# Copying the inverse transform's result out of PSUM on ScalarE, and pairing the products with q

## The chip, the core and the metric

The kernel runs on one core of one Trainium2 chip. The metric is the device time of one execution in microseconds (us); smaller is better. The kernel before was run eight times: the median is 303.95 us, the lowest 302.06, the highest 305.27. One of these runs, of 302.5 us, was recorded by the hardware profiler.

A core has five engines that run their own instruction streams and meet at semaphores: TensorE (PE in the profile; its weight loads are PEld), VectorE (DVE), ScalarE (ACT), GpSimd (POOL) and SyncE (SP). Transfers are issued from the streams of SyncE, ScalarE and GpSimd.

## The reference, cut to what matters

S is 2048 rows, D is 640 columns, F is 1728; all data are bf16.

```
def _A_ref(q, k, v, shift_k, ssm_k, ssm_D):     # q comes in layer-normed
    k_shift = sum of k shifted by t = 0..3 rows, each times a tap shift_k[:, 3 - t]
    kv = k_shift * v
    y = irfft(rfft(kv padded to 2S) * rfft(ssm_k padded to 2S))[:S]    # causal convolution along the rows
    y = y + kv * ssm_D
    return q * y

def _B_ref(x, w_gate, w_up, w_down):
    return (silu(x @ w_gate) * (x @ w_up)) @ w_down

h  = x + _A_ref(layernorm(x), k, v, shift_k, ssm_k, ssm_D)
h2 = h + _B_ref(layernorm(h), w_gate, w_up, w_down)
```

## The kernel before, in words

**Blocks and halves.** The 2048 rows are cut into four blocks, j = 0 to 3, of 512 rows. Inside a block a row's index is 4p + b: p is the partition (0 to 127), b the row group (0 to 3). The 640 columns are cut into two halves, c = 0 and 1, of CW = 320 columns, so that a half of one row group is one fp32 PSUM tile of 128x320.

**The convolution** is computed block by block in a frequency domain. Block 0 uses dense tables (`dense_c`): forward products of the filter's rows (dfK) and of kv (dfX), a complex product on VectorE (`products`, `combine`), and inverse products (di) which leave the result of two row groups in two PSUM tiles each. Blocks 1 to 3 (`conv_c`) use a two-stage transform: first stage (s1), shuffle by DMA (sh), second stage (s2), complex products with earlier blocks' spectra, inverse second stage (i2), shuffle (rs), inverse first stage (i1). Nearly every TensorE result is copied out of PSUM by `evac`, which may run on ScalarE or VectorE.

**The end of the convolution** is `conv_bp` (lines 1144 to 1166), run for every block, half and pair of row groups `bp`: 16 times. It writes the normalised q rows of two row groups into a tile `qt`, multiplies them by the convolution's result, which stands in PSUM (one product for each row group, line 1153 for block 0, where the scale is applied too, line 1160 for the others), adds both row groups to the rows x in one instruction of 640 columns (line 1164), and takes the statistics for the second layer norm (line 1166, `ln_stats`).

**The FFN.** `ln_bp` normalises the rows (L1006 on VectorE or L1007 on ScalarE) and turns them (line 1199, on TensorE for blocks 0 and 1; by a transposing DMA for blocks 2 and 3). `ffn_f` makes gate and up products, 512 columns wide, for 14 slices of F; `ffn_b` makes the down products, 320 columns wide.

**The shifted k** is made in `kv_block`: four products of the k rows with the four taps (`mul`), added up on VectorE, and the product with v. Each instruction works on four row groups, 1280 columns. Product 0 needs the block's own rows; products 1 to 3 need also three leading rows before each partition's four. For block 0 these are loaded by `load_front` (lines 755 to 783) into `KIN0`: the main rows, cell "m", in one transfer from ScalarE's queue, and the leading rows, cell "h", in two transfers from SyncE's queue (partitions 16 to 127 and 1 to 15). The filter's rows of block 0 (`kraw0c`) come from SyncE's queue too and are turned by TensorE (`k_turn`, line 798).

**What sets the order.** The program records operations with the tiles' cells that they read and write (`Prog.op`). `Prog.schedule` places them on the engines one after the other by readiness and priority; the priorities are the ranks in `_ORDER` (lines 16 to 64), a written list of all operation numbers, and `_WHO` forces an operation that could run on either to ScalarE ("a") or VectorE ("d"). What comes out is a fixed order for every engine and queue. PSUM has eight tiles of 512 fp32 columns: three for the FFN ("pF") and five for the rest ("pC"). A tile can be written again when its last reader is done.

The profile gives most instructions the line of a helper: L681 is a matmul, L664, L665, L667 and L668 are PSUM copies (L664 and L667 on ScalarE, L665 and L668 on VectorE, the last of each with a scale), L672 a transfer, L891 a VectorE tensor_tensor, L997 the power in the layer norm's rstd on GpSimd.

Of the kernel before, what the change touches and what calls it, by code (L numbers as in the profile page):

```python
# [16 lines left out]
59 1571 1566 12 3 1574 93 71 61 1575 1570 73 57 75 67 1567 1535 1534 1538 1586 1551 1203 53 1562 1526 63 1550 1558 1539 1530 1590 1599 1614 1594 6  # L17
1555 1603 1554 1559 1546 1563 1591 1609 1605 1582 1600 1527 84 9 82 137 169 143 145 91 131 102 1531 1543 407 108 151 421 153 90 69 65 100 99 135 160
147 417 409 149 411 419 141 139 162 1585 1604 1601 413 1608 1595 1583 1596 1592 382 1542 122 1610 105 383 386 384 380 1578 119 44 81 158 111 1612 433
211 209 313 78 77 621 449 448 381 95 223 155 393 387 186 232 185 157 414 117 144 152 98 96 138 150 408 221 473 439 136 410 188 109 146 262 412 148 190  # L20
189 83 140 531 40 527 820 573 526 446 477 480 521 41 120 103 62 55 33 74 76 94 58 17 19 1587 1581 114 1613 173 172 511 509 85 164 68 113 528 176 165
460 470 422 512 516 515 514 1547 543 268 517 467 523 469 215 212 216 167 66 35 92 371 174 175 42 106 400 370 166 118 156 385 479 438 415 206 376 192
197 201 193 315 191 401 177 397 529 525 154 101 418 142 182 115 112 471 39 437 38 183 21 273 48 45 10 171 116 121 195 461 459 373 389 178 416 87 16
510 54 168 395 1406 236 202 259 260 133 36 159 198 204 22 196 60 261 513 184 97 0 170 181 72 399 161 420 124 123 402 396 88 234 233 379 37 89 129 64
70 5 14 369 4 7 163 110 28 451 278 454 388 519 434 368 269 398 132 24 179 187 52 372 390 107 545 450 1410 27 25 8 551 1408 1404 764 1418 1426 751 11
194 18 1174 1416 263 256 244 180 31 541 539 303 80 126 435 441 235 283 427 429 47 46 128 465 79 127 1353 1350 86 391 34 483 255 252 23 284 225 537 486
547 306 463 104 26 582 325 227 226 242 29 773 228 32 30 803 377 1252 258 229 253 423 205 43 125 231 50 49 51 264 591 134 1381 213 218 13 466 797 199
207 1382 1251 220 476 214 475 540 222 430 798 200 447 219 203 600 617 643 564 834 311 224 723 431 320 291 506 575 503 568 572 1007 1 285 508 501 474
806 498 272 496 560 668 487 488 953 305 1244 210 1264 505 275 633 1254 337 987 355 394 862 276 628 1256 281 812 814 271 507 570 604 596 296 818 598
295 286 630 810 266 618 310 612 607 876 955 1268 663 1119 580 578 956 631 290 550 1165 577 15 2 1169 1412 499 816 208 392 375 270 436 532 428 468 472  # L30
524 237 217 453 462 442 485 538 542 546 491 481 673 586 1378 1510 655 484 455 544 456 622 280 1520 957 367 795 432 999 552 558 548 440 1109 321 464
920 265 452 518 1248 522 530 627 863 374 592 287 297 579 1258 1009 917 1266 693 799 282 802 1001 1262 944 669 492 609 562 590 566 500 300 494 56 20
327 848 769 444 443 378 497 520 307 808 574 277 245 230 826 445 770 767 1130 968 951 832 1173 1133 240 1015 915 914 243 251 326 974 614 960 856 615
301 585 1227 619 553 536 533 406 424 404 403 594 254 241 819 565 778 602 257 1179 830 426 425 238 713 828 535 583 316 250 334 860 964 1094 1310 490
489 239 405 836 712 707 844 942 1025 783 784 976 554 1092 775 1427 1313 1312 457 1311 534 249 996 776 774 366 841 1083 1068 880 348 978 842 821 768
697 692 1222 555 949 939 247 248 246 274 664 688 708 1060 940 938 677 1022 717 1066 1063 1108 1070 722 1069 796 936 682 947 727 854 329 1037 1036 916
925 1067 932 667 638 636 635 322 567 809 815 1170 1166 1132 962 926 929 1377 927 1026 1011 1005 804 1013 728 931 1020 1231 718 879 1218 1472 924 975
928 1225 1228 933 1012 1124 1078 1354 1419 1144 1349 1290 995 1017 624 866 864 1053 1003 1573 1343 1253 678 1355 1464 946 1260 771 807 559 1113 557
1016 1114 674 1090 1107 1105 1271 805 1272 1129 1141 1458 549 1557 921 292 1606 1456 1549 1580 1569 1462 1588 1593 458 824 1014 587 772 1376 685 793
715 1267 1134 1451 789 1433 1120 794 1018 1615 1584 1401 1403 730 1019 1220 822 1470 1500 1457 792 786 935 788 710 1236 1045 679 1505 1512 1118 881  # L40
714 1317 1273 1513 1511 1178 1415 1235 1440 1187 1503 1239 1508 937 1436 1504 606 952 1116 576 1430 1466 1428 1460 1438 1414 1536 1151 1540 683 347
130 1360 1229 1216 288 997 1448 1315 1006 1142 1226 1522 1117 1523 902 904 1072 726 556 1345 1323 1320 1309 1319 781 1387 1468 877 588 1021 1380 1352
1171 672 1465 1461 1217 782 1177 1154 721 1279 1137 1145 1153 1010 1351 1407 1519 1277 1443 1136 1284 1084 1245 1517 813 684 493 1224 1219 811 504
1265 725 780 972 779 1192 1205 1367 1445 1269 1000 922 1243 843 1242 1241 765 1405 1342 1158 875 1532 1347 620 675 1167 823 716 652 918 734 1399 1064
1041 1579 1495 1560 1556 998 357 923 977 1391 1073 1287 1327 695 1413 1435 1331 747 1112 1493 919 752 1337 1335 1329 1087 676 1223 1299 694 339 748
1123 1373 1291 646 777 1385 671 1307 1221 1397 1389 1285 1122 1409 1402 1270 1027 1043 739 1479 330 954 858 686 1425 743 1131 1143 1086 689 761 1121
1111 1449 1484 1358 1147 1155 1055 1489 1568 1305 738 1076 312 343 1411 1237 1234 1197 984 1446 1474 1156 1359 1471 1431 365 970 1463 658 699 703 900
611 1429 1238 1370 1024 698 966 719 892 980 352 898 660 648 1280 704 1276 599 874 852 657 838 1322 1341 495 1049 1030 502 1292 1293 1033 1450 1469
1368 1452 1082 1240 1184 1577 1518 988 894 896 1497 1363 1364 1477 1475 1476 1051 1398 1157 691 1288 709 1097 1388 666 1442 1437 1396 1149 1128 736
1274 1372 1029 1176 1441 1492 1161 1125 1362 1498 1483 1163 1496 1598 1490 846 1194 681 1275 1190 662 982 1079 1421 994 645 1023 711 705 608 605 1289  # L50
1056 1420 650 361 701 724 1099 1032 1031 309 1052 1281 696 1048 1028 700 1050 943 1059 1494 1193 571 279 1164 1366 318 790 690 1502 589 561 890 1509
1371 878 1507 1196 1152 1482 1375 1140 1374 1189 1333 1038 629 909 1160 886 1480 906 1369 1162 1175 1297 986 1393 1417 641 1499 1200 1439 1054 1127
1453 569 593 1209 1213 1057 1047 1395 1361 1447 1139 642 706 1004 1075 1303 1195 1148 1365 745 1392 1286 934 563 597 1294 1394 1278 1390 1283 1062 702
1040 687 298 289 293 948 945 1039 835 1065 1061 616 1058 1473 1035 1301 756 1295 299 1126 1186 910 1198 869 1501 656 1146 644 1506 1491 868 653 1247
639 871 640 637 1081 1080 887 888 1250 850 872 905 911 908 882 654 1138 833 1042 294 847 595 482 581 829 827 478 845 744 584 304 733 1302 853 855 601
800 613 323 308 1478 907 314 1296 1304 1246 1467 1459 603 867 1211 328 324 1521 1071 735 961 1172 884 885 1100 1386 1089 839 651 625 1597 1282 737
1074 941 746 634 1214 1210 1002 1384 732 731 755 356 1095 1102 1093 973 831 825 1168 1348 1101 1110 1106 1383 1516 319 632 362 959 963 817 837 670
1255 990 665 1257 338 992 1259 967 1541 363 360 623 1098 358 341 344 754 965 1249 883 1328 340 1553 1183 1201 267 912 930 1379 913 1135 1565 801 317
1611 1561 1602 1537 647 359 849 851 785 1545 1529 950 1103 1104 1346 958 865 857 1344 1339 1316 1115 873 891 333 787 1008 840 659 1485 979 1552 1544
1564 1528 1481 1576 1572 903 1336 1199 859 899 971 720 729 1207 861 1159 680 1180 1326 1091 1334 1298 753 983 981 1044 1088 1096 626 610 302 331 985  # L60
969 870 1261 791 901 1321 1318 889 364 346 1185 895 353 332 649 349 342 893 1548 1208 1077 740 1202 1212 1182 1181 760 993 1488 1444 1085 1314 1191
1204 1330 1046 1306 1300 1308 897 345 335 350 1533 354 762 1423 1356 1607 742 758 1150 1263 661 989 991 351 336 1432 1338 1616 1332 1340 1034 1230
1233 1215 1424 1434 1422 1324 757 1589 1514 766 1455 1325 741 1400 750 749 759 1487 1232 1525 1515 1486 1454 1524 1357 1206 1188 763
"""
_WHO = (
# [456 lines left out]
def bass_sequential_preLN__ssm_conv_h3__swiglu_ffn__prompt_kernel(  # L522
# [6 lines left out]
    R = 4  # L529
# [836 lines left out]
```

## Time and profile before

| | us |
|---|---|
| median of eight runs | 303.95 |
| the profiled execution | 302.5 |
| its span, first to last instruction | 300.7 |
| TensorE busy, matmuls | 278.9 |
| VectorE busy | 240.6 |
| ScalarE busy | 194.1 |
| GpSimd busy | 33.5 |

The granted TensorE clock is 0.994 of full speed over the span. Data moved by DMA: 43.24 MB.

The page shows, in this order: busy time of each engine; the span in 40 slices of 7.5 us with the busy share in tenths; the chain of work that ended last, followed back from the last instruction; and the costliest groups of instructions, each with its count, its busy time, the mean ns of one and the idle time before it. Other views answer from the same recorded execution: busy time for any stretch of the span, the timeline of one engine with its idle times in brackets, and the groups with every shape apart. An engine's neighbouring instructions overlap by their pipelines, so the duration of one can be longer than the spacing of two that queue.

### The profile page before, as it was taken

The page shows a single profiled execution, that of the slowest core. Times are in us where ns is not written, and L with a number is a line of the kernel's source. Part 1 is how long each engine was busy: PE and PEld are TensorE (multiplying, and loading weights), DVE is VectorE, ACT ScalarE, POOL GpSimd, SP SyncE. Part 2 cuts the span into 40 slices and gives each one's busy share as a digit, 9 for nine tenths or more (in the row PEclk, how much of TensorE's full clock was granted, in tenths as well). Part 3 has the DMA queues.
Part 4 walks back from the last instruction along what each step waited for, and adds up shares of the span by engine and source line. Part 5 has one row for each costly group of instructions (what it writes and reads, how often), then busy time and mean ns, then how long its engine had stood idle before and what let it go on. Part 6 is the DMA issues. An engine that isn't in the chain of part 4 may idle for free.

```text
span 300.7 us, 5136 instructions
## 1 busy us (share of the span) xinstructions
PE 278.9 (93%) x1786; PEld 151.7 (50%) x1804; DVE 240.6 (80%) x486; ACT 194.1 (65%) x457; POOL 33.5 (11%) x34
## 2 busy tenths in 40 slices
PE   3798897799999989999989999999998999999996
PEld 1465564444543466664433456654444576444564
DVE  3899899998899989999989999984689872323322
ACT  5298899897776857998979985867976010332100
POOL 2103300401101114110160000200030010000000
PEclk9999999799999999999999999999999999999999
DMA  7999997634944796595443204644101124000011
GB/s 215 361 379 342 355 354 240 203 65 158 231 140 116 168 269 191 113 266 173 131 87 83 94 23 143 165 132 156 42 2 44 46 53 122 2 0 0 2 44 44
DMA packets 42472, 43.24 MB, mean 144 GB/s; under 512 B 14848, under 2 KB 37056, under 8 KB 42320
## 3 DMA queue, kind: packets, MB, share of 16 engines
q1 hardware_dynamic: 38974, 38.30, 40.4%
q0 software_dynamic: 3328, 3.97, 8.2%
q10 hardware_dynamic: 146, 0.66, 0.6%
q8 instruction: 14, 0.23, 0.3%
q14 instruction: 10, 0.08, 0.1%
HBM read 20.63 MB, written 2.62 MB: 77 GB/s over the span
## 4 chain that ended last, share of the span: by engine, by line
PE 50%; DVE 35%; DMA 4%; issue 3%; POOL 3%; ACT 2%; SPq 1%; DVEq 0%; ACTq 0%
PE ps L681 49%; DVE sb L891 30%; DMA sb<-sb 3%; POOL stt L997 3%; DVE stt L981 2%; DMA sb<-in_A_ssm_k_dram 2%; DVE sb L665 2%; DVE sb L1153 1%; ACT sb L664 1%; PE ps L1199 1%; ACT sb L1007 1%; SPq L672 1%; ACT sb L667 1%; PE ps L798 0%; DVE sb L1006 0%
## 5 line engine op out<-in xcount | busy, mean ns | idle before, releaser
L681 PE MATMUL ps<-sb 128*128 128x320 bf16 (+2 forms) x1186 | 222.4, 338 | 11.0 <-DMA sb<-in_A_shift_k_dram 2.3
L891 DVE TENSOR_TENSOR sb<-sb 128x1280 bf16<-128x1280 bf16 (+3 forms) x270 | 165.6, 672 | 1.2 <-ACT sb L667 0.8
L681 PEld LDWEIGHTS ps<-sb 128*128 128x128 bf16 (+2 forms) x1204 | 114.3, 99 | 102.2 <-DVE sb L891 5.4
L664 ACT ACTIVATE sb<-ps 128x320 bf16<-128x320 f32 (+2 forms) x257 | 104.2, 482 | 28.5 <-PE ps L681 21.4
L891 DVE TENSOR_TENSOR sb<-ps,sb 128x320 bf16<-128x320 f32 (+2 forms) x70 | 38.9, 572 | 42.6 <-PE ps L681 27.6
L681 PE MATMUL ps<-sb,tab 128*128 128x320 bf16 (+2 forms) x512 | 66.5, 306 | 3.6 <-ACT sb L664 1.7
L1225 ACT ACTIVATE sb<-ps 128x512 bf16<-128x512 f32 (+1 forms) x56 | 33.6, 601 | 37.8 <-PE ps L681 37.3
L681 PEld LDWEIGHTS ps<-sb,tab 128*128 128x128 f16 (+2 forms) x512 | 32.0, 101 | 36.5 <-issue 13.4
L1007 ACT ACTIVATE sb<-sb,stt 128x320 bf16<-128x320 bf16 (+1 forms) x36 | 25.1, 731 | 14.8 <-DVE stt L999 13.4
L997 POOL TENSOR_TENSOR stt<-stt 128x2 f32<-128x2 f32 (+1 forms) x12 | 16.1, 1345 | 115.7 <-DVE stt L996 79.9
L1067 POOL DMA_DIRECT2D sb<-sb x12 | 12.2, 1014 | 74.2 <-DVE sb L891 61.8
L667 ACT ACTIVATE sb<-ps 128x320 bf16<-128x320 f32 x42 | 15.7, 445 | 4.8 <-PE ps L681 4.7
L665 DVE CAST sb<-ps 128x320 bf16<-128x320 f32 x29 | 13.4, 481 | 5.5 <-PE ps L681 5.5
L981 DVE BATCH_NORM_STATS2 stt<-sb 128x6 f32<-128x320 bf16 x32 | 14.3, 477 | 0.0
L1027 ACT ACTIVATE sb<-sb,stt 128x640 bf16<-128x640 bf16 x16 | 13.2, 827 | 0.2
L1020 ACT ACTIVATE sb<-sb 128x640 bf16<-128x640 bf16 x16 | 12.0, 748 | 0.1
L798 PE MATMUL ps<-sb 128*128 128x128 bf16 (+1 forms) x48 | 4.0, 231 | 3.4 <-DMA sb<-in_A_ssm_k_dram 2.3
L809 POOL TENSOR_TENSOR sb<-sb 1x320 bf16<-1x320 bf16 x2 | 3.6, 1796 | 21.4 <-ACT sb L664 14.6
L798 PEld LDWEIGHTS ps<-sb 128*128 128x128 bf16 (+1 forms) x48 | 3.2, 120 | 5.0 <-DMA sb<-in_A_ssm_k_dram 2.9
L1006 DVE TENSOR_SCALAR sb<-sb,stt 128x320 bf16<-128x320 bf16 (+1 forms) x12 | 4.6, 400 | 0.1
L1199 PE MATMUL ps<-sb 128*128 128x128 bf16 x40 | 3.8, 242 | 1.0 <-DVE sb L1006 1.0
L999 DVE TENSOR_TENSOR stt<-stt 128x2 f32<-128x2 f32 (+1 forms) x12 | 1.8, 148 | 3.1 <-POOL stt L997 3.1
(23 smaller groups left out, 29.5 us busy)
## 6 DMA issues: line engine op xcount, KB each, us to landing
sb<-sb SPq DMA_DIRECT2D x72, 160.0 KB, 2.2
sb<-sb POOLq DMA_DIRECT2D x12, 320.0 KB, 4.4
out_dram<-sb SPq DMA_DIRECT2D x16, 160.0 KB, 1.8
sb<-in_A_k_dram SPq DMA_DIRECT2D x8, 280.0 KB, 4.6
sb<-in_B_w_down_dram SPq DMA_DIRECT2D x13, 160.0 KB, 6.3
sb<-cst_den SPq DMA_DIRECT2D x8, 256.0 KB, 6.4
sb<-in_A_v_dram SPq DMA_DIRECT2D x6, 320.0 KB, 3.9
sb<-in_A_q_dram SPq DMA_DIRECT2D x6, 320.0 KB, 3.7
```

The source lines that it names most:

```text
L664: fns = {"act": lambda a: a.activation(out=dst(), in_=src(), func=ACTF.Copy), "dve": lambda v: v.tensor_copy(out=dst(), in_=src())}
L665: "dve": lambda v: v.tensor_copy(out=dst(), in_=src())}
L667: fns = {"act": lambda a: a.activation(out=dst(), in_=src(), func=ACTF.Copy, scale=scale), "dve": lambda v: v.tensor_scalar(out=dst(), in0 ...
L681: return lambda t: t.matmul(o(), l(), r(), start=st, stop=sp)
L891: return lambda v: v.tensor_tensor(out=o(), in0=a(), in1=b_(), op=op)
L981: vec(dve1(CW, False), lambda v: v.bn_stats(st6(l, j, b, c), V(xt, b * D + c * CW, CW)), [(xt, (b, c))], [(ST, ("s", l, j, b, c))], prio, ...
L997: P.op({"pool": 1.2}, lambda g: g.tensor_tensor(out=y, in0=va, in1=stt[:, 420:420 + hi - lo], op=ALU.pow), c1 + [(ST, "half")], c3, prio, ...
L1007: "act": lambda a: a.activation(out=dst(), in_=src(), func=ACTF.Identity, scale=rs(l, j, b), bias=tmv(l, j, 3)[:, b:b + 1])},
L1020: P.op({"act": act_c(D) + 0.22}, lambda a, b=b, jt=jt: a.activation(out=V(jt, 0, D), in_=V(xt, b * D, D), func=ACTF.Copy, accum_out=tmv(l, ...
L1027: P.op({"act": act_c(D) + 0.3}, lambda a, b=b, jt=jt: a.activation(out=V(jt, 0, D), in_=V(xt, b * D, D), func=ACTF.Square, bias=tmv(l, j, ...
L1067: P.op({"pool": 1.35}, [lambda g: g.dma_start(v4(t0), src(), accum_op=ALU.add)], [(t0, 0)] + cells, [(t0, 0)], prio, dma=(2.1, 2.1, 0.8), ...
L1225: P.op({"act": act_c(n)}, lambda a: a.activation(out=dst(), in_=src(), func=ACTF.Silu), rd, wr, -1000, name=f"si{nm}", after=after)
```

## The change

In `conv_bp` the product with q no longer reads PSUM. Each of the two PSUM results is copied by ScalarE to bf16 (for block 0 with the scale), into SBUF that is free by then: `KIN0` for block 0, the shuffled tile `HTt` for the others. Then one VectorE instruction multiplies both row groups, 640 columns, from SBUF. In `load_front` the main and the leading k rows of block 0 are each loaded in two column halves, with cells for each half, so that the products of half 0 depend on half 0 alone. SyncE issues four transfers for the leading rows, ScalarE two for the main rows; pieces are 640 bytes long. `_ORDER` and `_WHO` are replaced by new lists for the new set of operations; the lists are left out here.

```
-            dma([kin(0, 128, 3, 7)], 655, [], [(KIN0, "m")], -2001, name="kin0", w=2.6, eng="act")
-            dma([kin(16, 128, 0, 3), kin(1, 16, 0, 3)], 490, [], [(KIN0, "h")], -2000, name="kin0h", w=2.0)
+            dma([kin(16, 128, 0, 3, 0), kin(1, 16, 0, 3, 0)], 245, [], [(KIN0, "h0")], -2002, name="kin0h", w=1.1)
+            for c in range(2):
+                dma([kin(0, 128, 3, 7, c)], 328, [], [(KIN0, f"m{c}")], -2001 + 2 * c, name=f"kin0", w=1.4, eng="act")
+            dma([kin(16, 128, 0, 3, 1), kin(1, 16, 0, 3, 1)], 245, [], [(KIN0, "h1")], -2000, name="kin0h", w=1.1)
...
+            ot, ob, os_ = (KIN0, bp * 2 * D + c * CW, D) if ready else (HTt, bp * 4 * CW, 2 * CW)
             for k in range(2):
+                oc = [(ot, ("o", c, bp * 2 + k))]
                 if ready:
                     pk = [ready[k]]
-                    vec(dve1(CW), lambda v, k=k, pk=pk: v.scalar_tensor_tensor(out=V(qt, k * CW, CW), in0=B32(pk, 0, CW), scalar=SCALE, in1=V(qt, k * CW, CW),
-                                                                             op0=ALU.mult, op1=ALU.mult), tc(pk) + [(qt, k)], [(qt, k)], pr, name=f"o{j}{c}{bp}")
                 else:
...
-                    vec(dve1(CW), tt(lambda k=k: V(qt, k * CW, CW), lambda pk=pk: B32(pk, 0, CW), lambda k=k: V(qt, k * CW, CW), ALU.mult),
-                        tc(pk) + [(qt, k)], [(qt, k)], pr, name=f"o{j}{c}{bp}")
+                evac(lambda k=k: V(ot, ob + k * os_, CW), lambda pk=pk: B32(pk, 0, CW), CW, tc(pk), oc, pr, scale=SCALE if ready else None,
+                     name=f"oe{j}{c}{bp}", only="act")
+            vec(dve2(2 * CW), tt(lambda: V2(qt, 0, CW, 2, CW), lambda: V2(ot, ob, os_, 2, CW), lambda: V2(qt, 0, CW, 2, CW), ALU.mult),
+                [(ot, ("o", c, bp * 2 + k)) for k in range(2)] + [(qt, 0), (qt, 1)], [(qt, 0), (qt, 1)], pr, name=f"o{j}{c}{bp}")
```

## The prediction

> **What bounds the kernel now.** I read the page's engine shares and slices first, then busy time by stretch, then the chain that ended last, the groups with each shape apart, and VectorE's timeline of the first microseconds.
>
> ```profile
> PE 278.9 (93%) x1786; PEld 151.7 (50%) x1804; DVE 240.6 (80%) x486; ACT 194.1 (65%) x457; POOL 33.5 (11%) x34
> ...
> DVE  3899899998899989999989999984689872323322
> ACT  5298899897776857998979985867976010332100
> DMA  7999997634944796595443204644101124000011
> ```
>
> Up to about 175 us VectorE has no free slice, and the DMA engines are full up to about 50 us. TensorE looks busy everywhere, so its share says little; the stretches say more. I cut them at the first FFN product (60.78), at the first FFN product of block 2 (198.8) and at TensorE's last (297.6); the points come from matching the built program's order with the trace.
>
> ```profile
> core 0: us, PE busy (x) PEld busy (x) DVE busy (x) ACT busy (x) POOL busy (x), PEclk, DMA share, GB/s
> 0.00:9.20 9.20, 3.96 (x20) 1.76 (x20) 3.09 (x6) 4.32 (x10) 1.65 (x8) 1.00 0.77 224
> 9.20:60.78 51.58, 42.58 (x308) 27.00 (x308) 50.18 (x115) 42.95 (x106) 9.82 (x7) 0.97 0.96 320
> 60.78:198.80 138.02, 134.50 (x884) 70.44 (x892) 133.25 (x258) 111.83 (x269) 18.33 (x16) 1.00 0.56 145
> 198.80:297.60 98.80, 97.53 (x579) 52.52 (x585) 53.58 (x110) 34.96 (x74) 3.71 (x3) 1.00 0.14 44
> ```
>
> From 9.2 to 60.78 VectorE works 50.2 of 51.6 us. In gapless stretches late in the trace a 512-column matmul starts every 0.216 us and a 320-column one every 0.137 us. With those spacings TensorE's order holds 37.6 us of work ahead of the first FFN product and 223.5 us from it to the end. It starts that product at 60.78, so 23.2 us are lost before it; the rest takes 236.8 us, so 13.3 are lost after, 11.1 of them before 198.8 (126.9 us of work in 138.0). From 198.8 on, 96.6 us of work fill 98.8. So the end is: when FFN work begins, plus 223.5, plus what TensorE still loses. VectorE sets the first term.
>
> The chain that ended last gives the spacing of instructions that queue back to back:
>
> ```profile
> 49.43 0.78 DVE sb L891
> 50.21 1.20 DVE sb L1153 x3
> 51.41 0.40 DVE sb L891
> 51.81 0.40 DVE sb L1153
> ...
> 225.53 1.29 ACT sb L667 x4
> ```
>
> A 320-column product read from PSUM (L1153) costs VectorE 0.40 us, and so does the 640-column bf16 addition at 51.41; a copy on ScalarE costs 0.32. The durations are longer, since neighbours overlap:
>
> ```profile
> L664 ACT ACTIVATE sb<-ps 128x320 bf16<-128x320 f32 x219 | 83.8, 454 | 18.9 <-PE ps L681 17.8
> ...
> L891 DVE TENSOR_TENSOR sb<-sb 128x640 bf16<-128x640 bf16 x64 | 29.9, 481 | 0.1
> ...
> L665 DVE CAST sb<-ps 128x320 bf16<-128x320 f32 x29 | 13.4, 481 | 5.5 <-PE ps L681 5.5
> ...
> L1153 DVE SCALAR_TENSOR_TENSOR sb<-ps,sb 128x320 bf16<-128x320 f32 x8 | 3.6, 483 | 0.0
> ```
>
> **Part 1, the pair of row groups.** VectorE loses 32 products of 0.40 and gains 16 of 0.40: 6.4 us less. ScalarE gains 32 copies: 10.3 us at 0.32, 14.5 at 0.454. Of all PSUM copies of this shape VectorE keeps 32 of 35 and ScalarE takes 296 after 261.
>
> The Trainium skill speaks against part 1: "ScalarE: Activation LUTs", Rules for kernel authors, puts plain arithmetic on VectorE, in bf16 up to about three times faster. Going by that, the copy belongs on VectorE at a third of 454, 0.15 us; two copies and the product would cost it 0.70, still under the present 0.80, and ScalarE nothing. The rows deny it: VectorE's copy from PSUM takes 481 against ScalarE's 454 and is spaced 0.40, so two copies and a product would be 1.20. I go by the rows: only ScalarE makes it pay.
>
> **Part 2, the new order.** The order list is replaced whole, so I compared the built orders and added, along VectorE's, each kind's spacing (0.735 for 1280 columns, 0.40 for 640 or a PSUM read of 320, 0.23 for 320 in bf16). Up to VectorE's first normalised rows, which the first transposition for the FFN waits for (56.15), the sum falls from 47.4 to 44.0: four pairs -1.6, four PSUM copies given to ScalarE -1.6, one tap copy -0.4, a normalisation +0.3, the rest small. Up to the last copy before the first FFN product it falls from 51.3 to 46.8: two products of block 2 move behind it (-1.5), a copy comes ahead (+0.4). So -4.5 us. ScalarE's sum to that point goes from 42.2 to 41.5 and stays under VectorE's, so it is not the next bound there.
>
> TensorE's order holds 1.0 us less ahead of that product and 1.0 more behind it (224.5). From there to block 2's first, VectorE's sum goes from 131.8 to 127.2, ScalarE's from 103.6 to 106.7, TensorE's from 126.9 to 126.1. The 138.0 measured is 6 over VectorE's sum, so it could shorten by between 0 and 4.6; TensorE is nearly as full and follows waits, so I take 1.0.
>
> **Part 3, the first k rows.** VectorE's start now:
>
> ```profile
> 5.10 0.49 DVE L665 CAST sb<-ps 128x320 bf16<-128x320 f32 x1 [2.53 <-PE ps L681]
> 5.51 0.81 DVE L891 TENSOR_TENSOR sb<-sb 128x1280 bf16<-128x1280 bf16 x1
> 8.79 0.49 DVE L665 COPY sb<-ps 128x640 bf16<-128x640 bf16 x1 [2.47 <-PE ps L798]
> ```
>
> The 2.47 us wait is for filter rows that landed at 7.33. The second product stands behind it because the leading k rows landed at 9.11. With column halves the filter rows stand first in SP's queue, no 82 KB ahead, and 328 instead of 655 KB beside them on ScalarE's queue; the leading rows of half 0 are 244 KB. The second product moves ahead of the wait. That is worth 0.7 at least, and up to 2.3 if the filter rows land 1.6 sooner; a loss is bounded by the tap row, now second on ScalarE's queue (0.4). Pieces of 640 bytes take 34 ns against 203 for 5120, 1.3 times as long per byte: at most 0.5 us on a half. I take 1.0. SP issues two more transfers, some 1.0 us, while it runs far ahead of the landings.
>
> **The floor under this.** In both orders the loads amount to some 15.2 MB before the shuffles of block 1's first spectrum, which landed at 47.9 to 49.2 with the DMA engines full since 9 us. TensorE takes small products and 12 transposes (about 1.5 us) between them and the first FFN transposition, so that cannot come before about 50.7. I expect it at 56.15 - 3.4 - 1.0 = 51.75: just free of the floor.
>
> **GpSimd.** By the skill's "SBUF — State Buffer", Who interferes with whom, a VectorE instruction with two SBUF inputs shuts out a GpSimd one that reads SBUF. The trace agrees: L997 takes 2.93 us at 31.75, beside products from SBUF, and 0.70 at 54.09, beside statistics. The 16 new products have two SBUF inputs. By the rule each of 12 such steps could wait 0.40, 4.8 in all; but VectorE waits for GpSimd 3.1 us in all now, and pairing halves the number of these products. I count 0, within -0.5 and +1.
>
> **Sum.** First FFN product at 60.78 - 4.5 - 1.0 = 55.3; plus 224.5; plus 13.3 - 1.0 lost; the end of TensorE's work at 292.1 instead of 297.6: 5.5 us less. The profiled execution took 302.5 (span 300.7, 1.8 around it), so 297.0; the median of the runs, 303.95, lies 1.45 above it, so 298.45, say 298.5.
>
> **Rivals.**
> - The transfers hold the front: the filter rows of block 1 move from 8.9 to 12.8 MB down the queue (landed 30.0; a transfer at 13.0 MB landed at 40.8), and TensorE takes their transposes between the second and third inverse products of column half 1, at about 40. A late landing stalls TensorE, then VectorE. For it: the full DMA slices. Against: my expected times just clear. It leaves a gain of 1 to 3 us: 302.
> - The middle loosens as well: VectorE's 4.6 less counts almost whole. Against: TensorE has 126 us of work there. 295.
> - ScalarE's copies hold TensorE (slower): from 60.78 to 198.8, 16 of the copies stand in ScalarE's strict order while a PSUM bank is held, and VectorE's paired product waits for two of them. It decides when ScalarE, now 111.8 of 138.0 busy, has no free moment when a bank fills. 0.5 us at each of 16 is 8.0, which turns -5.5 into +2.5: 306.5. For it: its slices between 120 and 175 us are nearly full. Against: its order sum rises by only 3.1.
>
> **Chances.** Likeliest 0.52, transfers 0.20, looser middle 0.14, ScalarE 0.14. A measurement tells 0.5% from no change, 302.4 to 305.5. Of the transfers' case 0.12 lies below it and 0.08 within: faster 0.78, same 0.08, slower 0.14. The range, 294.5 to 304.0, takes in the middle's bound and the transfers' case and leaves out most of the slower one.
>
> **What would show it.** Right: the first FFN product at 54 to 57; VectorE's wait near 8 us gone or under 1.5; VectorE busy 5 to 8 us less in all, ScalarE 7 to 14 more; the 138 us stretch no longer than 138. Wrong: a stall of TensorE near 40 us on a DMA; more TensorE waits on ScalarE than the 10.3 us now (PE and its weight loads on L664); a wait for GpSimd above 4 us.

## The result and the profile after

| | before | after |
|---|---|---|
| median of the runs, us | 303.75 (32 runs, 301.89 to 305.95) | 298.96 (11 runs, 298.11 to 301.95) |
| ratio, 95% interval | | 0.9852 [0.9823, 0.9882] |
| profiled execution, us (span) | 302.5 (300.7) | 299.76 (297.9) |
| first FFN product, us | 60.78 | 59.48 |
| first FFN product of block 2, us | 198.8 | 194.8 |
| end of TensorE's work, us | 297.6 | 294.7 |

The change made the kernel faster by 4.8 us, 1.5%. Unless said otherwise, "after" is a profiled execution of the changed kernel at full granted clock, since an earlier one had 6.8 us of half clock in it, as we will see below. One run of the changed kernel beside the experiments, of 303.06 us, counts as slow (over 1.5% above the fastest) and is left out of the figures below.

The first view is the page's list of busy times, then the busy time of each engine in the same four stretches as in the prediction (boundaries moved with the three events in the table).

```profile
PE 276.7 (93%) x1785; PEld 152.0 (51%) x1804; DVE 235.5 (79%) x473; ACT 200.0 (67%) x486; POOL 35.6 (12%) x34
```

```profile
0.00:9.16 9.16, 3.82 (x20) 1.75 (x20) 3.11 (x6) 4.32 (x10) 1.71 (x8) 1.00 0.82 233
9.16:59.48 50.32, 42.05 (x300) 25.61 (x300) 46.00 (x104) 41.07 (x107) 9.22 (x5) 1.00 1.01 320
59.48:194.80 135.32, 131.50 (x873) 70.95 (x883) 129.97 (x252) 114.38 (x285) 21.68 (x18) 1.00 0.56 143
194.80:294.70 99.90, 98.97 (x595) 53.67 (x602) 55.88 (x113) 40.23 (x87) 2.98 (x3) 1.00 0.18 53
```

In the second stretch VectorE works 46.00 us where it worked 50.18: the order removed 4.2 us of its work ahead of the FFN, nearly what was counted. Yet the stretch is only 1.3 us shorter. VectorE's idle time in it rose from 1.4 to 4.3 us. The third stretch is 2.7 us shorter. The last is 1.1 longer; by the sums of the prediction it holds 1.8 us more of TensorE's work (224.5 - 126.1 = 98.4, against 96.6). The sum is -2.9 us at TensorE's end.

Even the 1.3 us is not won where the prediction had most of it. VectorE's first normalised rows, which the first FFN transposition waits for, start at the same time in the kernel before (L1006) and after (L1010):

```profile
55.65 0.45 DVE L1006 TENSOR_SCALAR sb<-sb,stt 128x640 bf16<-128x640 bf16 x1
```

```profile
55.67 0.45 DVE L1010 TENSOR_SCALAR sb<-sb,stt 128x640 bf16<-128x640 bf16 x1
```

From the first addition of products (10.05 before, 9.39 after) to these rows VectorE works 42.0 us instead of 44.4, but it waits 4.3 instead of 1.2.

The groups with each shape apart show the moved work. The 16 new products of 640 columns stand in the first line (64 before), the copies in the other two (219 and 42 before).

```profile
L895 DVE TENSOR_TENSOR sb<-sb 128x640 bf16<-128x640 bf16 x80 | 37.4, 481 | 2.1 <-ACT sb L665 1.8 <-ACT sb L668 0.2
...
L665 ACT ACTIVATE sb<-ps 128x320 bf16<-128x320 f32 x246 | 93.5, 461 | 21.8 <-PE ps L682 21.1
...
L668 ACT ACTIVATE sb<-ps 128x320 bf16<-128x320 f32 x50 | 19.1, 449 | 1.8 <-PE ps L682 1.7
```

**Where the front's gain went.** The longest idle time of VectorE between 9.2 us and the first FFN product can be followed through four engines. VectorE's timeline after, with the idle time before a piece and its releaser in brackets:

```profile
25.86 4.30 DVE L895 TENSOR_TENSOR sb<-sb 128x1280 bf16<-128x1280 bf16 x8
32.89 0.17 DVE L1000 TENSOR_SCALAR stt<-stt 128x4 f32<-128x4 f32 x1 [2.73 <-ACT sb L1031]
```

ScalarE's timeline, then TensorE's and GpSimd's:

```profile
31.61 0.44 ACT L665 ACTIVATE sb<-ps 128x320 bf16<-128x320 f32 x1 [3.39 <-PE ps L682]
31.95 0.82 ACT L1031 ACTIVATE sb<-sb,stt 128x640 bf16<-128x640 bf16 x1
```

```profile
30.86 8.32 PE L682 MATMUL ps<-sb 128*128 128x320 bf16 x60 [3.24 <-POOL sb L813]
```

```profile
25.75 5.06 POOL L813 TENSOR_TENSOR sb<-sb 1x320 bf16<-1x320 bf16 x1 [14.90 <-ACT sb L665]
```

Read backwards: VectorE waits for a statistics step of ScalarE; that step stands behind a copy of a product; the product waits for an addition on GpSimd. This is `d_add` (`name="dadd"`), which adds the D row to one row of the turned filter, 320 values on one partition, before the forward products of half 1. It takes 5.06 us and ends 0.65 us after VectorE's last product (30.16). In the kernel before the same addition took 2.38 us and TensorE waited 0.35 for it:

```profile
25.28 2.38 POOL L809 TENSOR_TENSOR sb<-sb 1x320 bf16<-1x320 bf16 x1 [14.63 <-ACT sb L664]
```

```profile
27.71 7.24 PE L681 MATMUL ps<-sb 128*128 128x320 bf16 x52 [0.35 <-POOL sb L809]
```

Its other instance, for half 0, took 1.22 us in both kernels. Why the two differ so is taken up at the end.

**The start.** VectorE's first work after:

```profile
7.51 1.56 DVE L895 TENSOR_TENSOR sb<-sb 128x1280 bf16<-128x1280 bf16 x2 [4.93 <-ACT sb L665]
8.98 0.48 DVE L666 COPY sb<-ps 128x640 bf16<-128x640 bf16 x1
9.39 3.00 DVE L895 TENSOR_TENSOR sb<-sb 128x1280 bf16<-128x1280 bf16 x3
```

The two waits of 2.53 and 2.47 us have become one of 4.93: the tap row now lands later, behind half of the main k rows on ScalarE's queue, so that TensorE's tap products wait 5.2 us for it instead of 2.3. The filter copy no longer waits, and the first addition of products starts at 9.39 instead of 10.05. Of these 0.66 us some 0.4 come from the tap copy (L665 at 5.10 before), which VectorE no longer makes.

**The clock.** The page's row of granted clock, by slices of 7.5 us, of the kernel before and of the earlier profile of the changed kernel (302.32 us):

```profile
PEclk9999999799999999999999999999999999999999
```

```profile
PEclk9999599999999999999999999999999999999999
```

In the trace these are stretches of 3.41 us, or two of them in a row, in which TensorE had half its clock. In the kernel before it is this one, with the stretch ahead of it (PEclk stands behind POOL's busy time):

```profile
52.37:55.78 3.41, 1.72 (x18) 0.92 (x17) 3.41 (x18) 2.63 (x8) 0.85 (x2) 1.00 0.40 150
55.78:59.19 3.41, 3.04 (x22) 1.68 (x22) 3.36 (x8) 3.41 (x8) 2.38 (x3) 0.50 0.82 253
```

The mean clock of each run tells how many such steps it had ahead of the last microseconds. All runs of the two kernels whose clock is on record, those beside the experiments among them, sorted by it:

| granted clock | steps of 3.41 us | before: runs, median | after: runs, median |
|---|---|---|---|
| 1.000 | 0 | none | 10, 298.7 |
| 0.994 | 1 | 12, 302.4 | 5, 300.0 |
| 0.989 | 2 | 13, 303.5 | 2, 302.1 |
| 0.983 | 3 | 15, 305.1 | none |

At one step each, the changed kernel is 2.4 us ahead, at two steps 1.4 (from two runs). The 2.7 us between the two profiled executions are no cleaner: the one of before had one step, the one after none. So about half of the 4.8 us, or less, is the gain at equal clock; the rest goes with the clock, since the changed kernel mostly runs with no such step, and the kernel before with one to three. An estimate: 3.41 us at half clock withhold at most 1.7 us of TensorE's time, so where two rows differ by 2.1, the step alone isn't all of it.

### The profile page after: what moved, and what is told of

The parts are those of the page before. It is cut to its first block, busy times and chain, and to the rows that moved or that the text cites. A ratio compares the mean times of both kernels' runs of the same rounds, so it can differ in the third digit from the quotient of the medians.

```text
span 300.5 us, 5153 instructions
## 1 busy us (share of the span) xinstructions
PE 279.6 (93%) x1785; PEld 153.4 (51%) x1804; DVE 235.4 (78%) x473; ACT 199.9 (67%) x486; POOL 35.6 (12%) x34
## 4 chain that ended last, share of the span: by engine, by line
PE 48%; DVE 22%; issue 13%; ACT 7%; POOL 5%; DMA 4%; SPq 0%; ACTq 0%; DVEq 0%; POOLq 0%
PE ps L682 48%; DVE sb L895 19%; ACT sb L665 3%; DMA sb<-sb 3%; ACT sb L1011 2%; POOL stt L1001 2%; POOL sb L813 2%; DVE sb L666 1%; DMA sb<-in_A_shift_k_dram 1%; DVE stt L985 1%; ACT sb L668 1%; DVE sb L1010 0%; ACT sb L1231 0%; POOL sb L1071 0%; SPq L673 0%
## 5 line engine op out<-in xcount | busy, mean ns | idle before, releaser
L895 DVE TENSOR_TENSOR sb<-sb 128x1280 bf16<-128x1280 bf16 (+3 forms) x286 | 172.1, 661 | 12.4 <-ACT sb L665 9.3
L665 ACT ACTIVATE sb<-ps 128x320 bf16<-128x320 f32 (+1 forms) x283 | 113.5, 489 | 29.7 <-PE ps L682 24.1
L682 PE MATMUL ps<-sb,tab 128*128 128x320 bf16 (+2 forms) x512 | 63.5, 302 | 2.2 <-ACT sb L665 0.8
L895 DVE TENSOR_TENSOR sb<-ps,sb 128x512 bf16<-128x512 f32 (+2 forms) x46 | 28.1, 618 | 42.6 <-PE ps L682 34.8
L1011 ACT ACTIVATE sb<-sb,stt 128x320 bf16<-128x320 bf16 (+1 forms) x31 | 22.1, 741 | 10.6 <-DVE stt L1003 8.1
L668 ACT ACTIVATE sb<-ps 128x320 bf16<-128x320 f32 x50 | 19.1, 449 | 1.8 <-PE ps L682 1.7
L813 POOL TENSOR_TENSOR sb<-sb 1x320 bf16<-1x320 bf16 x2 | 6.3, 3135 | 22.4 <-ACT sb L665 15.2
L1010 DVE TENSOR_SCALAR sb<-sb,stt 128x320 bf16<-128x320 bf16 (+1 forms) x17 | 6.6, 414 | 0.3
L1000 DVE TENSOR_SCALAR stt<-stt 128x2 f32<-128x2 f32 (+1 forms) x12 | 1.9, 159 | 3.3 <-ACT sb L1031 3.3
L1031 ACT ACTIVATION_READ_ACCUMULATOR sb<-sb,stt 128x1 f32 x16 | 3.8, 239 | 0.0
```

Of the source, the lines that this page charges most:

```text
L665: fns = {"act": lambda a: a.activation(out=dst(), in_=src(), func=ACTF.Copy), "dve": lambda v: v.tensor_copy(out=dst(), in_=src())}
L668: fns = {"act": lambda a: a.activation(out=dst(), in_=src(), func=ACTF.Copy, scale=scale), "dve": lambda v: v.tensor_scalar(out=dst(), in0 ...
L682: return lambda t: t.matmul(o(), l(), r(), start=st, stop=sp)
L813: P.op({"pool": 1.0}, lambda g: g.tensor_tensor(out=V(kt, 0, CW, 0, 1), in0=V(kt, 0, CW, 0, 1), in1=V(DROW, c * CW, CW, 0, 1), op=ALU.add) ...
L895: return lambda v: v.tensor_tensor(out=o(), in0=a(), in1=b_(), op=op)
L1011: "act": lambda a: a.activation(out=dst(), in_=src(), func=ACTF.Identity, scale=rs(l, j, b), bias=tmv(l, j, 3)[:, b:b + 1])},
```

## The experiments

Each is a full kernel. The order of work on each engine is written down and held, save for the instructions that an edit adds, drops or moves. All were timed beside the kernel before; ratios are to it.

**1. The changed kernel once more.** No edit.

> The changed kernel itself, for a second recorded execution: the first was among its slowest (302.3 us at a granted clock of 0.987, where most of its runs took 298.1 to 299.8). Theory of the prediction (less VectorE work ahead of the first FFN product): at a full clock that product starts at 55 to 58 us and the run takes 299. Rival (the front gained nothing; the stretch from the first FFN product to block 2's is what shrank): it starts at 60 us or later in this execution too, the stretch takes 133 to 135 us instead of 138.0, and the run takes 299 just the same.

299.76 us (298.52 to 300.17), ratio 0.988 [0.984, 0.992]. The lines above are from this run. The first FFN product at 59.48 misses the 55 to 58 of the theory; the stretch behind it, 135.3, lies just outside the rival's 133 to 135. The rival comes nearer: most of the gain is in that stretch. In the earlier profile, with two steps of half clock near 30 us, that product came at 62.75 and the stretch took 134.6.

**2. The pairing alone.** The kernel before with part 1; the two products become one at the place of the later, each copy stands in ScalarE's order at the moment its result was ready.

```
-                    vec(dve1(CW), tt(lambda k=k: V(qt, k * CW, CW), lambda pk=pk: B32(pk, 0, CW), lambda k=k: V(qt, k * CW, CW), ALU.mult),
...
+                evac(lambda k=k: V(ot, ob + k * os_, CW), lambda pk=pk: B32(pk, 0, CW), CW, tc(pk), oc, pr, scale=SCALE if ready else None,
...
+            vec(dve2(2 * CW), tt(lambda: V2(qt, 0, CW, 2, CW), lambda: V2(ot, ob, os_, 2, CW), lambda: V2(qt, 0, CW, 2, CW), ALU.mult),
```

> Part 1 alone: the order of the kernel before is kept on every engine; the 32 copies are put into ScalarE's order where the inverse's result is ready, and the paired product stands where the later of the two products stood. The k rows are loaded whole. Theory of the prediction: VectorE is 6.4 us shorter, 1.6 of it ahead of the first FFN product and about 3 more in the stretch behind it: 300.5 to 302.5. Rival (only the rewritten order pays): 303 to 305. Rival (ScalarE's copies hold up TensorE): 305 to 308.

307.7 us, ratio 1.015 [1.010, 1.019]: slower. VectorE's timeline of this kernel shows the price; each line begins with a paired product, and what follows it on the same helper line is counted in. The first is block 1's half 0:

```profile
85.40 1.70 DVE L891 TENSOR_TENSOR sb<-sb 128x640 bf16<-128x640 bf16 x4 [2.47 <-ACT sb L664]
114.44 1.70 DVE L891 TENSOR_TENSOR sb<-sb 128x640 bf16<-128x640 bf16 x4 [3.18 <-ACT sb L664]
```

Before, the four products at this place started at 81.17, 81.68, 82.32 and 82.73, each as its bank came. Now the first pair needs both banks and both copies: its last inverse product ends at 83.6, the last two copies start at 84.92 and 85.24 behind others on ScalarE, and the product starts at 85.40. In the list of waits VectorE's L891 waits 12.7 us in all for copies of ScalarE's L664, a line that the list of before doesn't have, and the stretch from the first FFN product to block 2's takes 141.2 us instead of 138.0. It isn't the clock: at 0.989 this kernel has 307.5, the one before 303.5. The time lies in the range of the second rival, that ScalarE's copies hold up TensorE. That is a smaller part of it by the waits: TensorE's for L664 grew from 10.3 us to 13.8 (PE and weight loads), VectorE's from nothing to 12.7.

**3. Pairing alone, paired products moved back.** The code of 2, with VectorE's list changed at four places: the paired products of block 0 half 1 (first pair), block 1 half 0 (first pair) and half 1 (second pair), and block 2 half 1 (first pair), with what depends on them, stand behind 0.9, 2.5, 3.2 and 1.2 us of VectorE work that doesn't. Block 0's copies stand just ahead of their use in ScalarE's list.

```
-o100, o101, h100, h101
+(2.5 us of other work), o100, o101, h100, h101
```

> Part 1 alone in the order of the kernel before, as in pair_alone (307.7), but with the places chosen for it: four of the paired products, with what depends on them, move behind independent VectorE work that is as long as VectorE waited there (0.9, 2.5, 3.2 and 1.2 us), and the copies for block 0 stand just ahead of their use. Theory (the paired product puts the inverse product, two copies and two hops in front of VectorE, and only an order made for it hides that): 301 to 304, most of the loss gone. Rival (ScalarE's extra copies are the loss): 306 to 308 as before.

310.98 us, ratio 1.024 [1.020, 1.028]: slower still, outside the theory's range and the rival's. My theory of the wait alone fell. Waits as long return before paired products (2.98 us at 88.76, 3.09 at 118.81), and the first FFN product comes at 64.6 (62.5 in experiment 2; this profile had three steps of half clock ahead of it, that one two, so the difference is not the order's alone). This local repair of the order doesn't do; what a better one would give was not tried.

**4. The order alone.** The changed kernel with its order and its k halves, but the products as before, one each, straight from PSUM. Seven inverse products had to be moved to where q is ready, since their banks would not be free otherwise.

```
-                evac(lambda k=k: V(ot, ob + k * os_, CW), lambda pk=pk: B32(pk, 0, CW), CW, tc(pk), oc, pr, scale=SCALE if ready else None,
...
+                    vec(dve1(CW), tt(lambda k=k: V(qt, k * CW, CW), lambda pk=pk: B32(pk, 0, CW), lambda k=k: V(qt, k * CW, CW), ALU.mult),
```

> Parts 2 and 3 without part 1: the changed kernel's order and k loads, but each row group's result is multiplied straight from PSUM, two products on VectorE near the places where the copies stood. Seven of the inverse products of blocks 2 and 3 had to move back to where the q rows are normalised, since nothing else frees their PSUM tile. Theory of the prediction: VectorE gets the 6.4 us back, and the run takes 302.5 to 305.5. Rival (the rewritten order pays by itself): 299 to 300.5.

307.88 us, ratio 1.016 [1.011, 1.021]: slower as well, above both ranges, by 3.0 us at a clock of 0.989. Because of the seven moves it is not quite the order by itself. First FFN product at 64.0, the stretch after it 137.5; its profile has two steps of half clock near 30 us, as the earlier one of the changed kernel, which had 62.75 and 134.6. TensorE's weight loads wait 13.0 us for VectorE's L895, against 7.0 in the changed kernel. The addition on GpSimd takes 5.04 us here, so its length comes with the order, not with the pairing.

**5. The copies on VectorE.** The changed kernel with

```
-                     name=f"oe{j}{c}{bp}", only="act")
+                     name=f"oe{j}{c}{bp}", only="dve")
```

> The changed kernel with its 32 copies on VectorE instead of ScalarE, at the same moments of the order. By the spacing of VectorE's PSUM copies (0.40 us), which the prediction took: VectorE has 12.8 us more, of which 3.2 lie ahead of the first FFN product and some 6 in the stretch behind it, where it was as full as TensorE: 305 to 309. By the rule that a copy on VectorE costs a third (0.15 us): 4.8 us more and no wait for ScalarE: 299 to 301.

311.62 us, ratio 1.028 [1.023, 1.032]. Against 298.96 that is 12.7 us for 32 copies, 0.40 each; between runs of equal clock (0.994) it is 10.1, 0.32 each. It is slower than the 305 to 309 of the theory, and far from the 299 to 301 of the rival. The price by the rows of before (0.40) is near, and not the 0.15. That estimate stretched the row in "ScalarE: Activation LUTs", Rules for kernel authors: its threefold speed is for bf16 and operations with a single source, and this copy reads fp32 from PSUM.

**6. The taps first.** The changed kernel with another beginning of ScalarE's order (the main k rows are m0 and m1):

```
-m1, tap row, table load, m0
+tap row, m0, table load, m1
```

> The changed kernel with ScalarE's four first operations in the order of use: tap row, main rows of half 0, the table-load activation, main rows of half 1. The changed order has half 1 first, then the tap row (landed near 5.1 us instead of 2.3), then the activation, then half 0 (landed at 7.7). Theory: the missing start is this order; the first product comes at 5 to 5.5 instead of 7.5, TensorE's first filter product about 1 us earlier, and all that follows 1 to 2 us: 297 to 298.5. Rival (the front is held further on, by the addition on GpSimd or by the transfers): the first product comes sooner, the first FFN product does not, and the run takes 299 to 300.

301.0 us, ratio 0.989 [0.986, 0.993]: no gain. At a clock of 1.00 its four runs have a median of 300.7, the changed kernel's ten 298.7, so it is 2.0 us slower, above both ranges. TensorE's timeline, with idle time and releaser:

```profile
2.47 1.86 PE L682 MATMUL ps<-sb 1*128 1x320 bf16 x6 [2.47 <-DMA sb<-in_A_shift_k_dram]
...
11.36 9.36 PE L682 MATMUL ps<-sb 128*128 128x320 bf16 x48 [3.35 <-DMA sb<-cst_den]
31.61 8.32 PE L682 MATMUL ps<-sb 128*128 128x320 bf16 x60 [3.24 <-POOL sb L813]
```

The tap products start 2.7 us sooner, but the filter's products then wait for their tables, which are transfers too, and the addition on GpSimd costs the same 3.24 us. VectorE's first product starts at 7.59, now waiting for the k rows, and its first addition at 9.47 (7.51 and 9.39 in the changed kernel). So the late tap row costs nothing at the start: what is behind it is late as well. Part of the loss is in the front, where the first FFN product comes at 60.4 instead of 59.48; the rest is open.

**7. The D-row addition on VectorE.** The changed kernel with

```
-            P.op({"pool": 1.0}, lambda g: g.tensor_tensor(out=V(kt, 0, CW, 0, 1), in0=V(kt, 0, CW, 0, 1),
+            P.op({"dve": 0.3}, lambda g: g.tensor_tensor(out=V(kt, 0, CW, 0, 1), in0=V(kt, 0, CW, 0, 1),
```

> The changed kernel with the addition of the D row to the filter's first row (320 columns on one partition, twice) on VectorE instead of GpSimd. On GpSimd the second took 5.06 us beside VectorE's products (2.37 in the kernel before), and TensorE stood 3.6 us behind it. Theory (GpSimd is shut out by VectorE's reads, and the front waits for it): the gap near 28 us goes, the first FFN product comes at 56 to 57.5 instead of 59.5, and the run takes 296 to 298. Rival (something else is due just behind it): 298.5 to 300.

297.05 us (296.83 to 297.92), ratio 0.977 [0.974, 0.981]: the lowest median of all. VectorE's timeline shows the second addition among the products:

```profile
22.77 3.87 DVE L895 TENSOR_TENSOR sb<-sb 128x640 bf16<-128x640 bf16 x9
26.55 0.30 DVE L813 TENSOR_TENSOR sb<-sb 1x320 bf16<-1x320 bf16 x1
26.79 3.55 DVE L895 TENSOR_TENSOR sb<-sb 128x320 bf16<-128x320 bf16 x7
30.27 0.15 DVE L1000 TENSOR_SCALAR stt<-stt 128x4 f32<-128x4 f32 x1
```

0.30 us instead of 5.06, and L1000 starts at 30.27 with no wait instead of 32.89. TensorE's products of half 1 begin at 27.4 instead of 30.9, VectorE's first normalised rows at 53.74 instead of 55.67, the first FFN product at 57.6 instead of 59.5. All six runs have a granted clock of 1.00.

**8. Both.** Experiments 6 and 7 together.

> Both edits, the order of use on ScalarE's queue and the addition on VectorE. Theory: the first FFN product comes at 54.5 to 56.5, near where the prediction had it, and the run takes 294.5 to 297. Rival (the transfers of the front hold it: the shuffles before the first FFN product cannot land before about 49): no better than the addition alone.

297.55 us, ratio 0.978 [0.975, 0.982], first FFN product at 57.0: as 7 within the intervals. The theory (54.5 to 56.5, and up to 297 us) missed; the rival has the figures, but whether the transfers are what holds the front now was not tested.

**9. The addition on VectorE in the kernel before.** The edit of 7 on the kernel before.

> The kernel before with the two additions of the D row (1 x 320) on VectorE instead of GpSimd. Theory, that the addition became a cost through the new order, where products with two SBUF inputs stand back to back beside it (5.06 us there, 2.37 here): at most 1 us is won here, a median of 302.5 to 303.8, and the first FFN product moves by less than 1 us from 60.8. Rival, that the addition on GpSimd costs the same in every order: 2 us or more, as in the changed kernel, 301 to 302, the first FFN product near 58.8.

305.24 us, ratio 1.004 [1.001, 1.007]: no gain, a small loss, and not by the clock (304.4 against 303.5 at 0.989, 305.9 against 305.1 at 0.983). My theory said a small gain; the rival, a gain of 2, is out. The likely reason, not tested further: in the old order the addition stands on the engine that sets the first FFN product, and its place is a poor one, since VectorE waits there for ScalarE's copy of the filter:

```profile
25.42 0.31 DVE L809 TENSOR_TENSOR sb<-sb 1x320 bf16<-1x320 bf16 x1 [1.04 <-ACT sb L664]
```

**10 and 11. The first k rows whole.** The changed kernel with part 3 undone (taps, then the main rows in one transfer; the leading rows in one), without and with the edit of 7.

```
-            dma([kin(16, 128, 0, 3, 0), kin(1, 16, 0, 3, 0)], 245, [], [(KIN0, "h0")], -2002, name="kin0h", w=1.1)
...
+            dma([kin(0, 128, 3, 7)], 655, [], [(KIN0, "m")], -2001, name="kin0", w=2.6, eng="act")
+            dma([kin(16, 128, 0, 3), kin(1, 16, 0, 3)], 490, [], [(KIN0, "h")], -2000, name="kin0h", w=2.0)
```

> The changed kernel with its pairing and its order of work, but with the first k rows loaded whole as before (taps first on ScalarE's queue, then the main rows in one transfer; the leading rows in one). Theory, that the additions on GpSimd hold the front and the column halves are worth nothing while they do: 299.5 to 301.5, as with the taps first (301.0), the first FFN product at 60 to 61. Rival, that the halves carry about 1 us as the prediction had it: 300.5 to 302, the first FFN product 61 or later.

300.91 us, ratio 0.990 [0.984, 0.995], within both ranges.

> The same with the two additions of the D row on VectorE. Theory, that with GpSimd out of the way the front follows VectorE, whose second product then waits for the whole leading rows (9.1 instead of 6.4): 298.2 to 299.5, about 1 to 1.5 us over the same kernel with halves (297.1 and 297.6), the first FFN product at 58.5 to 59.5. Rival, that the halves are never worth anything: 297 to 297.7, the first FFN product at 57 to 58.

297.58 us, ratio 0.979 [0.975, 0.984]: the rival's range, with the theory's first FFN product. That product comes at 61.8 (60.4 with halves and the taps first) and at 58.6 (57.0): 1.4 and 1.6 us later in the profiled executions. The medians don't show it: 300.91 beside 301.0, and 297.58 beside 297.55. Against the change as it stands, without and with the edit of 7, that product is 2.3 and 1.0 us later, and the medians are higher by 1.5 (300.2 beside 298.7, runs at a clock of 1.00) and 0.5. The four runs behind the 300.2 spread over 2.4 us. So the worth of part 3 stays open, between 0 and some 2 us.

## Why the total was right and some of its terms were not

**Part 1, VectorE's and ScalarE's prices: right.** VectorE does 5.1 us less in all (5 to 8 was said) and 4.2 of the 4.5 ahead of the FFN. The 35 copies that ScalarE has more of this shape, 32 of them the new ones, add 13.1 us (10.3 to 14.5 was said for the 32). ScalarE as a whole does only 5.9 more, and the 7 to 14 was missed: the new lists give 5 normalisations to VectorE (L1007: 36 before, L1011: 31 after) and shift other work. Experiment 5 prices a copy on VectorE at 0.32 to 0.40, near what the spacing said.

**The floor and the transfers: right.** No wait for a transfer stands near 40 us in TensorE's timeline; its longest between 31 and 57 us is 0.59, for ScalarE.

**The rival of ScalarE: wrong here, in part right in the old order.** TensorE waits 10.5 us for ScalarE's L665 (PEld 8.0, PE 2.5), 10.3 before. Experiment 2 has a part of the mechanism at its place: with the copies in the old order, the paired product waits for them. The new order escapes by spacing: block 2's first copies run at 140 to 151 us and their products at 171 to 173, so the PSUM banks are free some 20 to 30 us sooner than if they had waited for q.

**The middle: sized too small.** I took 1.0 of a bound of 4.6; the stretch became 2.7 us shorter. In the terms of the sum, the loss behind the first FFN product was to fall from 13.3 to 12.3; it fell to 10.7 (294.7 - 59.48 - 224.5).

**The front: the step that failed.** I had 60.78 - 4.5 - 1.0 = 55.3, and named 54 to 57 as the sign; it was 59.48. At VectorE's first normalised rows the sum had 3.4 + 1.0 = 4.4 us, and nothing of it is there (55.65 and 55.67). VectorE's shorter order was there; what I had wrong is that its waits would stay as they were. They grew by 3.1 us, to 4.3: 2.73 for the chain that ends in GpSimd's addition and 0.97 for a copy of ScalarE at 19.99, while 0.94 for L997 went. The step is "I count 0, within -0.5 and +1" for GpSimd. I had looked at the power steps (L997) alone, and not at the addition L809, for which TensorE already waited 2.8 (PEld) in the kernel before. The sign that I had named for it, a wait for GpSimd above 4 us, came, though as the sum of two waits and on TensorE; VectorE's own waits for GpSimd (L999, 3.1 us before) fell to 2.1:

```profile
PEld ps L682 <- POOL sb L813: 6.0, 2, 3.6
...
PE ps L682 <- POOL sb L813: 5.1, 2, 3.2
```

Taken off GpSimd (7), the front is 1.9 us shorter, and the median 1.6 at equal clock (298.7 to 297.05). So this much is shown by experiment. The other terms of the missing 4.4 are read from the timelines alone: the start brought 0.66 instead of 1.0 and the 0.4 of the tap copy, "VectorE's wait near 8 us" moved to 7.51 rather than away, and VectorE's work from there on fell by 2.4 where 3.0 were counted.

Behind the first normalised rows the order was to win 1.1 us more, and the first FFN product does come 1.3 us sooner after them (3.81 instead of 5.13). But in the profile of before that stretch ran at half clock (55.78 to 59.19), as the 0.97 in the prediction's own row of 9.20:60.78 tells. How much of the 1.3 is the order's stays open.

**The step from the trace to the median: wrong too, the other way.** I added the 1.45 us by which the median of before lay above its profiled execution. That distance goes with the clock: the profile had one step of half clock, the median run two. After, the median lies 0.8 below its profiled execution, though both have none. So the profiled execution won 2.7 us where 5.5 was said, its one step of half clock included, and the step to the median brought 2.3 more that I hadn't counted. That 298.5 came so near 298.96 is luck: two errors, of 2.8 and 2.3 us, offset each other.

**Neither part pays alone.** Each cost 1.5 to 1.6% alone (2 and 4), and together they won 1.5%. In the old order VectorE's product waits for the two copies behind the result (12.7 us in all in experiment 2). In the new order without pairing VectorE has its 6.4 us again (busy 242.0 us, against 235.5), and results have to stay in PSUM until q is there; the longer waits of TensorE for VectorE in experiment 4 fit that.

## What to carry to other kernels

Where copying to SBUF frees an engine to work on wider pieces, the product must be moved away from the copy in the same step, or its wait eats the gain. When one engine's work is packed more closely, look up every short instruction on the other engines beside it, above all those on GpSimd that TensorE waits for, and price them from their slowest instance. And compare medians with the granted clock beside them: a kernel can win by having fewer lulls on TensorE ahead of its long work.

## What was not expected of the hardware

- A 1 x 320 addition on GpSimd took 1.22, 2.38 or 5.06 us, according to what VectorE did beside it. The 5.06 us (25.75 to 30.81) lie beside gapless products with two SBUF inputs and end 0.65 us after the last of them. The 2.38 us of before end at 27.66, 0.73 us after VectorE began a copy from PSUM, which VectorE's timeline of before shows:

```profile
26.93 0.48 DVE L665 CAST sb<-ps 128x320 bf16<-128x320 f32 x1
27.33 1.41 DVE L891 TENSOR_TENSOR sb<-sb 128x1280 bf16<-128x1280 bf16 x2
```

  And beside the 1.22 us one, a product of VectorE took 1.29 us instead of 0.83. The Trainium skill, "SBUF — State Buffer", Who interferes with whom, says that a VectorE instruction with two SBUF inputs and a GpSimd instruction reading SBUF shut each other out, and that one with at most one SBUF input, certain two-port modes apart, does not; these times agree with it, and the length was the surprise. The addition ended 0.65 and 0.73 us after VectorE's products paused; if that is its own time, an estimate, some 0.7 us of work stretched sevenfold. That the shared access to SBUF is the cause is argued from these times, not shown: no run changed it alone.
- TensorE's clock falls to half for 3.41 us at a time after lulls in the front: in the kernel before at 55.8 us, after 3.41 us in which TensorE was busy for 1.72; in the earlier profile of the changed kernel at 30.2 us, after 1.30 of 3.41. From row to row the table above has 1.1 to 2.1 us for a step. In "TensorE: Matmul & The Clock Gate", Part 1, a free-running window of 3.4 us with an idle TensorE brings the half clock; the length agrees, but here the window was not idle, and in the profile at full clock one with 1.57 of 3.41 busy had no such effect. What decides is left open. The kernels in which TensorE has no such wait for GpSimd's second addition (7, 8 and 11) had no step in 18 runs; the kernel before with the same edit (9) had two or three in all its twelve.
